# GpSimd's product for the 64-step decay, moved from ahead of the first block's presets to the front of the first half unit

## The chip, the cores and the metric

The kernel runs on one core of one Trainium2 chip. The metric is the device time of one execution in microseconds (us). Three runs of the kernel before gave 900.84 to 903.03 us, with a median of 901.47 us.

## What is computed

A linear attention with decay feeds two feed-forward layers. The inputs have 4 batches, 8 heads, 768 time steps and a head width of 48.

```python
for t in range(S):
    cur = np.einsum('bhd,bhe->bhde', u[None] * kt, vt)
    y[:, :, t] = np.einsum('bhd,bhde->bhe', rt, state + cur)
    state = w[None, :, :, None] * state + np.einsum('bhd,bhe->bhde', kt, vt)
x = y as [3072 tokens, 384]
h = x @ w_in;  g = max(h, 0) + alpha * min(h, 0);  x = g @ w_out      # 384 -> 2048 -> 384
h = x @ w_in2; g = h * tanh(softplus(h));          out = g @ w_out2
```

## The kernel before

**The stages.** Time is cut into six blocks of 128 steps. A block over four batches makes 512 tokens, which is one block of the first feed-forward layer (`mA_h`, `mA_g`, `mA_hi`, `mA_lo`, `mA_out`, 16 slices of the hidden width each). All matrices are split into a high and a low part, and each product is made in three passes. The first block of the attention is worked in four whole units, one per batch (units 0 to 3). From unit 4 on, a unit is a half unit: 64 steps of two batches (`batch`). The second layer follows when all blocks of the first are done.

**A first unit u** goes through these steps. `prep_rk` scales r and k by powers of the decay (DVE). `c_first` makes the diagonal term (DVE, PE, and a copy `cc` on ACT, L385). `scores` makes k times r into two PSUM banks `sc` that all units share (PE, L432). `preset_first` writes the diagonal into a new tile A (POOL, L413). `masked` copies the scores above the diagonal over it (DVE, L436). `attend0` multiplies by v (PE, L447). `x_first` and `x_first_lo` split the result into `x` (ACT L154, DVE L157). `prep_kn` scales k for the state (POOL, L400), and `states_first` sums the states (PE, L509). The A tiles have two homes, so unit 2's waits for unit 0's to be read. The scores of a unit overwrite those that `masked` of the unit before it reads.

**The tables.** `tables` (L291) makes the powers `RK` on DVE. `load_RKs` (L328) copies them by four DMAs into `RKs`, with the heads in other seats. `RKs` is read by `prep_pair` (DVE, L370), which scales r and k of the half units, and by `tables_seat` (POOL, L326): one product of 112x4 elements. Its result `w64` is the decay of 64 steps. Only `t_decay` reads it (DVE, L491), first for unit 4.

```python
    def tables_seat():
        pool.tensor_tensor(out=w64, in0=RKs[:, 1, :, 0], in1=RKs[:, 0, :, HC + 1], op=ALU.mult)
...
        pool.affine_select(out=A_t[u].rearrange("s q p t -> s (q p) t"), in_=c_t[u][1].to_broadcast([128, H, C]),
...
        at(-100.4, tables_seat)
```

**What sets the order.** Each step is entered with `at(place, work)`. `run_plan` (L767) sorts all steps by place and issues them; the table `PLACES` (L59) replaces the place of the steps that it names. Every engine works through its own instructions in that order, so an instruction that waits holds up all behind it on its engine. SP issues the DMAs in the same way, with at most eight unfinished. `tables_seat` has no entry in the table, so its place is -100.4 (L843): behind `scale_Kn` (L336, -100.9) and ahead of `preset_first 1` (-99.35). Also on POOL are `prep_c` (L391, L392: the diagonal term of a half unit, whose sum over elements is `prep_c2` on DVE, L396), `half_tables` (L250, L252: tables for the half units, which overwrite the mask), the casts `w_hi` of every other weight slice (L197), and a memset of a column of the state T in `batch` (L467). `keep_warm` (L563) is filler on PE.

Of the kernel before, what the change touches and what calls it, by code (L numbers as in the profile page):

```python
# [53 lines left out]
def more_state(u):  # L54
# [30 lines left out]
    "load_unit 6": -5.5762, "w_scale (0,3)": -4.4549, "prep_kn 4": -4.4525, "prep_pair 4 1": -3.9618,  # L85
    "mA_h 1": -2.7838, "w_join (0,3)": -2.4808, "w_hi (0,2) False": -2.3395, "scores 4": -1.6028,
# [8 lines left out]
    "prep_c 6": 3.5188, "w_hi (0,5) True": 3.5446, "more_raw 9": 3.6703, "mA_h 4": 3.6974, "mA_out 2": 3.943,  # L95
    "w_lo (0,5)": 3.9878, "w_join (0,6)": 4.1777, "mA_hi 3": 4.1987, "prep_pair 6 1": 4.2457, "mA_lo 3": 4.2643,
    "mA_g 4": 4.3425, "more_raw 10": 4.4486, "w_scale (0,7)": 4.4891, "mA_hi 4": 4.6577, "w_join (0,7)": 4.7254,
    "w_hi (0,6) False": 4.845, "mA_lo 4": 4.9016, "masked 5 1": 5.0498, "w_hi (0,7) True": 5.081, "mA_h 5": 5.1059,
# [12 lines left out]
    "more_raw 14": 9.6065, "w_join (0,11)": 9.6182, "mA_g 9": 9.6854, "w_hi (0,11) True": 9.6935,  # L111
# [7 lines left out]
    "mA_h 12": 12.3428, "mA_g 12": 12.3703, "batch 7": 12.4094, "more_raw 16": 12.4248, "w_hi (0,13) True": 12.4403,  # L119
    "w_lo (0,13)": 12.6061, "w_hi (0,14) False": 12.7117, "mA_hi 12": 12.8951, "x_parts 7": 12.9656,  # L120
    "w_scale (0,15)": 13.0176, "mA_out 11": 13.1742, "mA_h 13": 13.2486, "w_lo (0,14)": 13.4007, "mA_h 14": 13.4763,
    "w_join (0,15)": 13.506, "w_hi (0,15) True": 13.7554, "mA_lo 12": 13.8955, "mA_g 13": 13.8982,
# [865 lines left out]
```

## Time and profile before

| what | value |
|---|---|
| median of three runs | 901.47 us (900.84 to 903.03) |
| the profiled execution's own time | 903.24 us |
| its span, first to last instruction | 901.5 us |
| TensorE busy | 877.4 us (97%) |
| VectorE, ScalarE, GpSimd busy | 632.3, 612.6, 97.0 us |
| mean granted clock of TensorE | 0.989 of full |

An engine's busy time is the time in which it has an instruction at work; for TensorE (PE) the ends of matmuls are modelled. "Granted clock" is the share of the full TensorE clock that the chip allowed. In the timeline, a row is one instruction or a merged run of them: start, length, engine, line, operation, output from input, and in brackets how long the engine was idle before it and what ended that.

### The profile page before, as it was taken

Reading aid. Unit: us, or ns where it says so; the run is one execution under the profiler, and the core shown is the slowest. Engines: PE = TensorE matmul, PEld = TensorE weight load, DVE = VectorE, ACT = ScalarE, POOL = GpSimd, SP = SyncE. Lnnn points to the kernel's source line nnn. Section 1 sums busy time; section 2 is a strip of 40 time slices with the busy share of each in tenths; the row PEclk is TensorE's granted clock in tenths of the full one; section 3 lists DMA queues with packets and bytes.
Section 4 is the critical chain, followed back from the end, with each engine's and each line's share of the span. In section 5 each row is a group of like instructions: output and inputs, shape, how many; then the busy total and the mean of one; then the engine's idle time right before and its main releaser. Section 6 shows DMA issues by size and latency. Waiting matters only on the chain.

```text
span 901.5 us, 17129 instructions
## 1 busy us (share of the span) xinstructions
PE 877.4 (97%) x6700; PEld 758.2 (84%) x6700; DVE 632.3 (70%) x1024; ACT 612.6 (68%) x1159; POOL 97.0 (11%) x119
## 2 busy tenths in 40 slices
PE   9389999999999999999999999999999999999998
PEld 8368878888888888888888899999989989998997
DVE  6198867656565665654665787787787787787875
ACT  2177656444554445543555798898898998998985
POOL 2352222111211122100001000000000000000000
PEclk9699999999999999999999999999999999999999
DMA  8933664435525525231431200200100100100100
GB/s 304 275 98 140 209 139 148 140 102 178 146 73 187 166 91 156 97 105 62 159 105 53 105 1 1 71 1 1 71 1 1 71 0 1 36 1 1 36 1 35
DMA packets 34016, 80.41 MB, mean 89 GB/s; under 512 B 5456, under 2 KB 21136, under 8 KB 33936
## 3 DMA queue, kind: packets, MB, share of 16 engines
q1 hardware_dynamic: 33520, 79.33, 27.8%
q8 instruction: 52, 0.85, 0.4%
q14 instruction: 28, 0.23, 0.1%
q10 hardware_dynamic: 416, 0.00, 0.0%
HBM read 61.16 MB, written 15.73 MB: 85 GB/s over the span
## 4 chain that ended last, share of the span: by engine, by line
PE 90%; DMA 3%; DVE 2%; SPq 2%; ACT 1%; issue 1%; POOL 0%; DVEq 0%; POOLq 0%; ACTq 0%
PE h L228 42%; PE acc L611 21%; PE acc L719 10%; PE sc L719 7%; PE yt L719 3%; PE sc L432 1%; DMA ubt<-in_ub 1%; PE sc L477 1%; PE h L463 1%; PE yt L484 1%; DMA RKs<-RK 1%; DMA w13u<-in_nat 1%; PE yt L463 1%; DMA nat<-in_nat 1%; SPq L552 0%
## 5 line engine op out<-in xcount | busy, mean ns | idle before, releaser
L228 PE MATMUL h<-x,w 128*128 128x512 f32 x1728 | 419.1, 392 | 3.0 <-DVE x L157 1.0
L228 PEld LDWEIGHTS h<-x,w 128*128 128x128 f32 x1728 | 323.5, 188 | 72.3 <-DVE w L157 1.6
L611 PE MATMUL acc<-ghi,w 128*128 128x512 f32 x516 | 175.2, 394 | 0.0
L579 ACT ACTIVATE m<-h 128x512 f32<-128x512 f32 x96 | 57.2, 595 | 91.3 <-PE h L228 91.2
L611 PEld LDWEIGHTS acc<-ghi,w 128*128 128x128 f32 x516 | 96.9, 188 | 21.5
L581 DVE SCALAR_TENSOR_TENSOR g<-m,oma,h 128x512 f32<-128x512 f32 x96 | 71.6, 746 | 58.7 <-ACT m L579 57.8
L154 ACT ACTIVATE ghi<-g 128x512 fp32r<-128x512 f32 x86 | 54.2, 630 | 80.3 <-PE acc L611 43.3
L611 PE MATMUL acc<-glo,w 128*128 128x512 f32 x258 | 101.0, 391 | 0.0
L157 DVE TENSOR_TENSOR glo<-g,ghi 128x512 fp32r<-128x512 f32 x86 | 60.2, 699 | 54.3 <-ACT ghi L154 54.2
L719 PE MATMUL acc<-w,ghiB 128*128 128x384 f32 x384 | 98.0, 337 | 0.0
L667 DVE SCALAR_TENSOR_TENSOR a<-ghi,h 128x512 f32<-128x512 f32 x96 | 66.1, 688 | 36.0 <-ACT ghi L664 28.9
L667 DVE SCALAR_TENSOR_TENSOR g<-s,c 128x512 f32<-128x512 f32 x96 | 66.3, 691 | 22.2 <-ACT s L664 19.0
L154 ACT ACTIVATE ghiB<-g 128x512 fp32r<-128x512 f32 x106 | 65.8, 621 | 18.6 <-DVE g L667 8.1
L157 DVE TENSOR_TENSOR gloB<-g,ghiB 128x512 fp32r<-128x512 f32 x106 | 72.7, 686 | 8.1 <-ACT ghiB L154 8.1
L675 ACT ACTIVATE m<-h 128x512 f32<-128x512 f32 x96 | 56.0, 583 | 28.1 <-PE h L228 28.1
L664 ACT ACTIVATE ghi<-m,half 128x512 f32<-128x512 f32 x96 | 69.6, 725 | 3.2
L719 PEld LDWEIGHTS acc<-w,ghiB 128*128 128x128 f32 x384 | 69.8, 188 | 1.3
L664 ACT ACTIVATE glo<-ghi,m 128x512 f32<-128x512 f32 x96 | 68.0, 709 | 0.1
L664 ACT ACTIVATE s<-glo,m 128x512 f32<-128x512 f32 x96 | 68.0, 709 | 0.0
L664 ACT ACTIVATE s<-s,m 128x512 f32<-128x512 f32 x96 | 68.0, 709 | 0.0
L667 DVE SCALAR_TENSOR_TENSOR b<-ghi,a 128x512 f32<-128x512 f32 x96 | 67.4, 702 | 0.1
L667 DVE SCALAR_TENSOR_TENSOR c<-glo,b 128x512 f32<-128x512 f32 x96 | 65.8, 685 | 0.0
(179 smaller groups left out, 1183.5 us busy)
## 6 DMA issues: line engine op xcount, KB each, us to landing
wrawr<-in_w SPq DMA_DIRECT2D x24, 768.0 KB, 6.0
nat<-in_nat SPq DMA_DIRECT2D x40, 288.0 KB, 4.4
w2d<-wj SPq DMA_DIRECT2D x16, 384.0 KB, 2.6
wraw<-w2d SPq DMA_DIRECT2D x16, 384.0 KB, 3.1
rk<-in_rkT SPq DMA_DIRECT2D x40, 128.0 KB, 2.9
x2d<-xo SPq DMA_DIRECT2D x6, 768.0 KB, 3.2
x<-x2d SPq DMA_DIRECT2D x6, 768.0 KB, 4.5
out<-oo SPq DMA_DIRECT2D x24, 192.0 KB, 1.9
```

The source lines that it names most:

```text
L154: act.activation(out=hi, in_=src, func=AF.Copy)
L157: eng.tensor_tensor(out=lo, in0=src, in1=hi.bitcast(F32), op=ALU.subtract)
L228: pe.matmul(h, w_in(layer, f, a, c), x[:, b, c, :], start=(k == 0), stop=(k == 3 * KC - 1))
L432: pe.matmul(sc_t[u][h][HALF[i], o], rk[ROWS[h], 1, j, s], rk[ROWS[h], 0, j, t], start=True, stop=True)
L463: pe.matmul(y[i][64 * q:64 * q + 64, p * HC:(p + 1) * HC], T[ROWS[h], 2 * bp + i, k, :], pair[i][ROWS[h], 0, k, t], start=(r == 0 and not ...
L579: act.activation(out=m, in_=hA[s], func=AF.Relu, scale=-1.0)
L581: dve.scalar_tensor_tensor(out=g, in0=m, scalar=oma[:, f:f + 1], in1=hA.pop(s), op0=ALU.mult, op1=ALU.add)
L611: pe.matmul(acc[0][c], w_out(0, f, a)[:, c * 128:(c + 1) * 128], g[b], start=(f == 0 and k == 0), stop=(f == NF - 1 and k == 2))
L664: act.activation(out=out, in_=in_, func=AF.Square, scale=scale, bias=fin[bias])
L667: dve.scalar_tensor_tensor(out=out, in0=in0, scalar=scalar, in1=in1, op0=op0, op1=ALU.mult)
L675: act.activation(out=bnew("t", n), in_=v["h", n], func=AF.Tanh, scale=0.5)
L719: pe.matmul(acc[1][t][:, :DM], g[a][:, t * C:(t + 1) * C], w_out(1, f, b), start=(f == 0 and k == 0), stop=(f == NF - 1 and k == 2))
```

## The change

`tables_seat` gets an entry in the table of places. The other rows of the table are only wrapped anew.

```diff
-    "w_scale (0,5)": 0.6537, "prep_c2 5": 0.6799, "masked 4 1": 0.6955, "mA_hi 0": 0.8517, "w_lo (0,2)": 1.0042,
-    "mA_lo 0": 1.3093, "mA_g 1": 1.3135, "batch 4": 1.5628, "t_decay 4": 1.7454, "w_scale (0,4)": 1.7967,
+    "tables_seat": 0.3, "w_scale (0,5)": 0.6537, "prep_c2 5": 0.6799, "masked 4 1": 0.6955, "mA_hi 0": 0.8517,
+    "w_lo (0,2)": 1.0042, "mA_lo 0": 1.3093, "mA_g 1": 1.3135, "batch 4": 1.5628, "t_decay 4": 1.7454,
...
```

GpSimd's (POOL's) instructions from the first preset on, before. L413 are the presets (each writes an A tile from its `cc`), L336 is `scale_Kn`, L326 the product, L400 `prep_kn`; the brackets hold the semaphores that an instruction waits for, DMAHW those of DMAs:

```order
L413 AFFINE_SELECT A<-cc 128x1024 [waits Activation_49]
L336 TENSOR_TENSOR m<-RK,w_98 112x512 [waits DVE_49]
L326 TENSOR_TENSOR w_91<-RKs 112x4 [waits DMAHW3_49,DMAHW4_49,DMAHW2_49,DMAHW1_49]
L413 AFFINE_SELECT A<-cc 128x1024 [waits Activation_49]
L400 TENSOR_TENSOR w11u<-w11u,Kn 128x384 [waits DMAHW0_49,Activation_49]
L413 AFFINE_SELECT A<-cc 128x1024 [waits DVE_49,PE_49,Pool_49]
```

The same place after the change:

```order
L413 AFFINE_SELECT A<-cc 128x1024 [waits Activation_49]
L336 TENSOR_TENSOR m<-RK,w_98 112x512 [waits DVE_49]
L413 AFFINE_SELECT A<-cc 128x1024 [waits Activation_49]
L400 TENSOR_TENSOR w11u<-w11u,Kn 128x384 [waits DMAHW0_49,Activation_49]
L413 AFFINE_SELECT A<-cc 128x1024 [waits DVE_49,PE_49,Pool_49]
L400 TENSOR_TENSOR w13u<-w13u,Kn 128x384 [waits DMAHW3_49]
```

The product with its wait for the four DMAs of `RKs` is gone from between the presets of unit 0 and unit 1; nothing else has changed places here.

Where the product stands now on GpSimd, at the first half unit (unit 4), after the change. L391 and L392 are `prep_c 5`, L197 is the cast of the weight slice (0,3), L467 the memset in `batch 4`, the second L400 `prep_kn 5`:

```order
L391 TENSOR_TENSOR nat<-nat,ubt 128x384 [waits DMAHW7_49,DMAHW0_49]
L392 TENSOR_TENSOR nat<-nat 128x384 [waits Pool_49]
L197 CAST w_592<-wj 128x768 [waits DVE_49,PE_49]
L326 TENSOR_TENSOR w_91<-RKs 112x4 [waits DMAHW3_49,DMAHW4_49,DMAHW2_49,DMAHW1_49]
L467 MEMSET T 112x8 [waits PE_49]
L400 TENSOR_TENSOR nat<-nat,Kn 128x384 [waits Pool_49]
```

It has come in between the cast and the memset. The instructions of PE, DVE, ACT and SP keep their order.

## Rows read from the trace of the kernel before

**Rows 1.** The page: the chain that ended last, by line.
```profile
PE h L228 42%; PE acc L611 21%; PE acc L719 10%; PE sc L719 7%; PE yt L719 3%; PE sc L432 1%; DMA ubt<-in_ub 1%; PE sc L477 1%; PE h L463 1%; PE yt L484 1%; DMA RKs<-RK 1%; DMA w13u<-in_nat 1%; PE yt L463 1%; DMA nat<-in_nat 1%; SPq L552 0%
```
**Rows 2.** Waits, 20 to 60 us: total us, times, longest us.
```profile
POOL w L326 <- DMA RKs<-RK: 18.9, 1, 18.9
DVE A L436 <- POOL A L413: 15.3, 1, 15.3
...
PE sc L432 <- DVE A L436: 13.7, 1, 13.7
```
**Rows 3.** Timeline of POOL: start us, us, what, idle before it.
```profile
13.51 2.00 POOL L336 TENSOR_TENSOR m<-RK,w 112x512 f32<-112x512 f32 x1
34.42 0.21 POOL L326 TENSOR_TENSOR w<-RKs 112x4 f32<-112x4 f32 x1 [18.91 <-DMA RKs<-RK]
34.57 1.09 POOL L413 TENSOR_SCALAR_AFFINE_SELECT A<-cc 128x1024 f32<-128x1024 f32 x1
...
37.64 0.99 POOL L400 TENSOR_TENSOR w13u<-w13u,Kn 128x384 f32<-128x384 f32 x1
...
43.99 1.71 POOL L391 TENSOR_TENSOR nat<-nat,ubt 128x384 f32<-128x384 f32 x1
45.78 1.00 POOL L392 TENSOR_TENSOR nat<-nat 128x384 f32<-128x384 f32 x1
...
59.24 0.11 POOL L467 MEMSET T<- 112x8 f32 x1 [0.31 <-PE yt L463]
```
**Rows 4.** Timeline of PE, units 0 to 3.
```profile
18.58 1.10 PE L432 MATMUL sc<-w10u 48*64 48x64 f32 x32
...
20.15 1.53 PE L447 MATMUL yt<-A,w9u 128*64 128x128 f32 x24
...
22.52 0.92 PE L563 MATMUL acc<-ghi 128*128 128x128 f32 x6
37.09 1.99 PE L432 MATMUL sc<-w12u 48*64 48x64 f32 x32 [13.65 <-DVE A L436]
39.01 2.83 PE L447 MATMUL acc<-A,w11u 128*64 128x128 f32 x24
...
44.46 1.10 PE L432 MATMUL sc<-w14u 48*64 48x64 f32 x32
```
**Rows 5.** Stretches on PE: length, busy, granted clock, DMA share, GB/s.
```profile
26.00:27.00 1.00, 0.00 (x0) 0.50 1.11 277
41.00:42.00 1.00, 1.00 (x12) 0.50 1.17 263
59.00:64.00 5.00, 4.55 (x157) 0.66 0.02 5
```
**Rows 6.** Timeline of ACT and DVE, units 0 to 4.
```profile
14.45 0.18 ACT L385 ACTIVATE cc<-acc 128x8 f32<-128x8 f32 x1 [2.38 <-PE acc L383]
...
19.49 0.95 DVE L186 SCALAR_TENSOR_TENSOR wj<-w4r 128x768 uint32<-128x768 uint32 x1
...
20.26 0.55 ACT L349 ACTIVATE Kn<-acc 128x192 f32<-128x192 f32 x2 [0.47 <-PE acc L346]
...
45.67 1.36 DVE L436 COPY_PREDICATED A<-cst,sc 128x512 f32<-128x512 uint32 x2 [0.82 <-PE sc L432]
...
49.71 0.54 DVE L396 TENSOR_REDUCE cc<-nat 128x8 f32<-128x384 f32 x1
...
54.01 0.89 ACT L180 ACTIVATE w7r<-w7r 128x768 f32<-128x768 f32 x1
```
**Rows 7.** The tile RKs, its readers: duration ns min/median/max, first and last start us.
```profile
L370 DVE TENSOR_TENSOR rk<-rk,RKs x20: 1217/1220/1586, 51.1 to 370.3; 112x1024 f32<-112x1024 f32 x20
```
**Rows 8.** DMA issues that began about 24.2 and 29.5 us: KB each, us to landing.
```profile
nat<-in_nat SPq DMA_DIRECT2D x1, 288.0 KB, 4.7
w7r<-in_w SPq DMA_DIRECT2D x1, 768.0 KB, 6.4
```
**Rows 9.** Chain of waits in order of time: start us, us, what.
```profile
66.31 2.04 PE h L228 x9
```

More of the change, by code (lines that the diff above doesn't have):

```diff
@@ L87 @@
     "more_raw 8": -1.1343, "mA_g 0": -0.9587, "masked 4 0": -0.7567, "prep_c 5": 0.0994, "w_hi (0,3) True": 0.1744,
[7 rows of a table removed]
[L95 to L98, printed above, removed]
[12 rows of a table removed]
-    "more_raw 14": 9.6065, "w_join (0,11)": 9.6182, "mA_g 9": 9.6854, "w_hi (0,11) True": 9.6935,
[7 rows of a table removed]
[L119 to L122, printed above, removed]
[7 rows of a table added]
+    "mA_g 3": 3.4249, "prep_c 6": 3.5188, "w_hi (0,5) True": 3.5446, "more_raw 9": 3.6703, "mA_h 4": 3.6974,
[9 rows of a table added]
+    "mA_out 5": 6.8918, "w_scale (0,10)": 7.2771, "w_hi (0,9) True": 7.378, "prep_kn 6": 7.475, "w_lo (0,8)": 7.4937,
+    "prep_c2 7": 7.5216, "mA_h 7": 7.5404, "mA_g 7": 7.6051, "w_lo (0,9)": 7.7949, "mA_hi 7": 7.8303,
+    "mA_out 6": 7.8692, "mA_lo 7": 7.8968, "masked 6 1": 7.9477, "preset 7 0": 7.9953, "mA_h 8": 8.0248,
+    "w_join (0,10)": 8.1006, "mA_g 8": 8.1678, "w_hi (0,10) False": 8.2945, "batch 6": 8.3841, "more_raw 13": 8.5179,
[7 rows of a table added]
+    "w_hi (0,12) False": 11.0336, "prep_kn 7": 11.1836, "mA_out 10": 11.2072, "w_scale (0,13)": 11.3063,
[3 rows of a table added]
+    "w_hi (0,13) True": 12.4403, "w_lo (0,13)": 12.6061, "w_hi (0,14) False": 12.7117, "mA_hi 12": 12.8951,
+    "x_parts 7": 12.9656, "w_scale (0,15)": 13.0176, "mA_out 11": 13.1742, "mA_h 13": 13.2486, "w_lo (0,14)": 13.4007,
+    "mA_h 14": 13.4763, "w_join (0,15)": 13.506, "w_hi (0,15) True": 13.7554, "mA_lo 12": 13.8955, "mA_g 13": 13.8982,
     "load_unit 9": 13.9017, "preset 8 1": 13.9928, "mA_out 12": 14.1785, "mA_hi 13": 14.2658, "masked 8 1": 14.2923,
```

48 rows, old and new, of the table PLACES are left out of this document.

## The prediction

> **What bounds the kernel now.** I read the page first. Its chain by line is nearly all PE, so a change off PE can pay only where PE stands still; but one of its rows is the DMA of RKs, with 1% of the span, about 9 us [rows 1]. Next come the waits of the first 60 us. The longest is POOL's: 18.9 us at L326, the product that the change moves, for that DMA. DVE then waits 15.3 us for a preset of POOL, and PE 13.7 us for DVE [rows 2]. These are not three losses but one, seen on three engines. The timeline of POOL shows how it begins: `scale_Kn` ends at 13.51 + 2.00 = 15.5 us, POOL stands until the product starts at 34.42, and only behind it, at 34.57, comes the preset of unit 1 [rows 3]. PE has finished its filler at 22.52 + 0.92 = 23.4 us and starts unit 2's scores at 37.09 [rows 4]. The product feeds nothing before unit 4. So a small instruction in an in-order queue holds up units 1, 2 and 3. A second loss hangs on it: 26 to 27 us, with PE idle, is granted 0.50 of the clock, and so is 41 to 42 us, when PE is busy again [rows 5]. [...]
>
> **The change, part by part.** No instruction and no DMA is added or taken away, and SP's queue is the same: the four DMAs of RKs are issued when they were. One POOL instruction of 0.21 us [rows 3] goes past three presets, the two `prep_c` and the other work of POOL up to the first half unit.
>
> *The old place.* The preset of unit 1 needs `cc`, ready at 14.45 + 0.18 = 14.6 us [rows 6], so it runs as soon as POOL is free, 15.5 to 16.6. `prep_kn 1` then waits for Kn, at 20.26 + 0.55 = 20.8 [rows 6], and takes 1.0 us as the like product does [rows 3]. On DVE, `masked 1` comes behind a weight step that ends at 19.49 + 0.95 = 20.4; with 1.36 us for the two copies (unit 3's, [rows 6]) it ends at 21.8. PE reaches the scores of unit 2 at 23.4. So the next to be late is nobody's data: **PE's own queue takes over**, with 1.6 us to spare on DVE.
>
> From here I replay PE with lengths at the full clock. Scores of unit 2, 23.4 + 1.1 = 24.5. `attend0 1`, 1.53, to 26.1. `attend0 2`, the same, to 27.6: its tile A became free when unit 0 was read, at 20.15 + 1.53 = 21.7, so its preset runs from about 21.9 to 23.0, and `masked 2` runs beside `attend0 1`, 24.5 to 25.9. Then filler, 0.92, to 28.5. The scores of unit 3 thus start at about 28.4, as merged rows overlap by 0.1, where they started at 44.46 [rows 4]. **That is 16.0 us earlier**: 13.7 us of standing still and 2.3 us from PE's clock (the scores and two `attend0` at half speed). From unit 3 on the order is the old one and most of it hangs on PE or on a full DVE queue, so I move it as a block by 16.0.
>
> *Does the block run into data that can't come earlier?* Four arrivals stay where they are. (1) RKs, seen on POOL at about 34.4 [rows 3]. `prep_pair` of unit 4 started at 51.1 [rows 7] and moves to 35.1: 0.7 us to spare, so this DMA alone caps the gain at 16.7. (2) The inputs of unit 4: the second half lands at 24.2 + 4.7 = 28.9 [rows 8]. `prep_c 4` would start at 43.99 - 16.0 = 28.0 and waits 0.9 us. Its two products last 46.78 - 43.99 = 2.8 us with the gap between [rows 3], so it ends at 31.7, and `prep_c2 4`, which reads it at 49.71 [rows 6], now wants it at 33.7. (3) The raw weights of slice 3 land at 29.5 + 6.4 = 35.9 [rows 8] and are first read at 54.01 - 16.0 = 38.0 [rows 6]. (4) The moved product is done long before `t_decay`.
>
> *The new place.* There the product finds RKs landed and costs 0.21 us. Behind it stands the memset of T, before which POOL was idle for 0.31 us waiting for PE [rows 3]: that idle time covers the product. Without this cover the memset would be 0.2 us later, and behind it PE's products with T.
>
> *What comes back.* POOL's presets and products again run beside a busy DVE. The trace shows a price of such company: `prep_pair` takes 1.22 us as a rule and 1.59 at most, 0.37 more [rows 7]. Most pairs merely move together; up to four new meetings, an estimate, are 1.5 us on DVE, against the 1.6 us of spare time there before unit 2. I take 0 and keep 1.5 for the range. [...]
>
> **Sum.** 0.0 (product) - 13.7 (idle) - 2.3 (clock) = -16.0 us, or -1.8%. Against its own execution: 903.24 - 16.0 = 887.2; that one lies 1.8 us above the median of the runs, so the median goes from 901.47 to **885.5 us**.
>
> The bounds. If PE had its half clock in this stretch all the same, only the idle time would go, 13.7 us: 887.8; with the 1.5 us of contention, 889.3. On the other side, RKs caps the move at 16.7. PE's clock falls once more near 61 us [rows 5], after waits for first weights and scores: 59 to 64 us have a mean clock of 0.66, which is 5 x 0.34 / 0.5 = 3.4 us at half speed [rows 5]; if this dip does not come again, up to half of it, 1.7 us, is won: 901.47 - 16.7 - 1.7 = 883.1. I widen this by 0.5 for the spread of medians: **882.6 to 889.8 us**.
>
> **The rivals.** I count over 0.3% (2.7 us), about what a measurement of this kernel can tell from no change, as a difference.
>
> *The supply takes over.* With everything 16 us earlier, the DMAs become what PE waits for. For it: 26 to 27 us and 41 to 42 us show the DMA engines full, a share above 1 [rows 5], and of the four arrivals one is missed by 0.9 us and one met by 0.7. Against it: the missed one has 2.0 us to spare at its reader. If each arrival came some 5 us later than I read it, the gain would be 11 us: about 890.5. Chance 0.06.
>
> *Slower: the clock stays down.* [...] Chance 0.02. [...]
>
> *Nothing is won.* POOL was not what held unit 1, and another input of the preset or of `masked 1` comes as late as RKs, or the gap opens again before the first slices. Against it: `cc`, the scores and POOL are all there by 20 us [rows 3, 4, 6]. 901.5. Chance 0.02.
>
> **How the numbers follow.** Forecast 0.90, supply 0.06, slower 0.02, nothing 0.02. The first two are faster by over 0.3%, 0.96 together; same 0.02; slower 0.02. The range holds most of the forecast's chance and a part of the supply's.
>
> **What would show it.** In the profile after, the preset of unit 1 starts at about 15.5 us and POOL's long wait for RKs is gone; PE has no gap at 24 to 37 us, and its granted clock stays full there; the scores of unit 3 start near 28.4 and take 1.10 us; `prep_pair` of unit 4 starts near 35, and only there may RKs appear as a releaser, on DVE. The product, at about 43 us, waits for nothing. The replay is wrong if PE waits for `masked 1` after 23.4, and the block's move is wrong if the first slice of the first feed-forward layer or a later landmark has gained other than 16 us. A dip of the clock near 44 to 47 us, in place of that at 61, would say that the dip moved along.

## The result, and the profile after

The median went from 902.19 us (900.84 to 903.03, four runs: the three known before and one more) to **887.77 us** (886.63 to 888.96, four runs). The ratio is 0.9842 with an interval of 0.9822 to 0.9861, so 14.4 us are won where 16.0 were forecast. The median lies inside the forecast range of 882.6 to 889.8 us and 2.3 us above the 885.5 named there; 0.7 us of this is the median of before, which the fourth run moved. Two later measurements of the same kernel gave 888.13 us (0.9840) and 888.35 us (0.9847).

| what | before | after |
|---|---|---|
| the profiled execution's own time | 903.24 us | 888.96 us |
| its span | 901.5 us | 887.2 us |
| TensorE busy | 877.4 us | 875.1 us (99%) |
| span less TensorE busy | 24.1 us | 12.1 us |
| VectorE, ScalarE, GpSimd busy | 632.3, 612.6, 97.0 us | 634.4, 612.7, 95.5 us |
| mean granted clock of TensorE | 0.989 | 0.998 |

The page's chain by line answers to [rows 1]. The DMA of RKs is gone from it; the DMAs that it now shows each carry 1 or 2%.

```profile
PE h L228 41%; PE acc L611 20%; PE acc L719 11%; PE sc L719 8%; PE yt L719 3%; DMA wrawr<-in_w 2%; DMA w6r<-in_w 1%; DMA nat<-in_nat 1%; SPq L552 1%; PE sc L432 1%; SPq L259 1%; PE sc L477 1%; PE h L463 1%; DMA w12u<-in_rkT 1%; PE yt L484 1%
```

POOL's timeline after, to be held against [rows 3]:

```profile
13.21 2.00 POOL L336 TENSOR_TENSOR m<-RK,w 112x512 f32<-112x512 f32 x1
15.17 1.09 POOL L413 TENSOR_SCALAR_AFFINE_SELECT A<-cc 128x1024 f32<-128x1024 f32 x1
20.92 1.00 POOL L400 TENSOR_TENSOR w11u<-w11u,Kn 128x384 f32<-128x384 f32 x1 [4.66 <-ACT Kn L349]
...
29.00 1.00 POOL L391 TENSOR_TENSOR nat<-nat,ubt 128x384 f32<-128x384 f32 x1 [0.84 <-DMA nat<-in_nat]
...
42.82 0.21 POOL L326 TENSOR_TENSOR w<-RKs 112x4 f32<-112x4 f32 x1
43.17 0.11 POOL L467 MEMSET T<- 112x8 f32 x1
```

The preset of unit 1 follows `scale_Kn` at once, at 15.17 us in place of 34.57, and the product waits for nothing at 42.82. PE's timeline, against [rows 4], shows what the early preset does, and then something new:

```profile
23.39 1.10 PE L432 MATMUL sc<-w12u 48*64 48x64 f32 x32
24.43 1.53 PE L447 MATMUL acc<-A,w11u 128*64 128x128 f32 x24
...
28.33 1.10 PE L432 MATMUL sc<-w14u 48*64 48x64 f32 x32
...
45.38 0.22 PE L484 MATMUL yt<-Ah,nat 64*48 64x64 f32 x1
47.52 0.21 PE L484 MATMUL yt<-Ah,nat 64*48 64x64 f32 x1 [1.93 <-issue]
...
48.63 0.52 PE L611 MATMUL acc<-ghi,w 128*128 128x512 f32 x1
48.96 0.61 PE L611 MATMUL acc<-glo,w 128*128 128x512 f32 x1
```

The scores of units 2 and 3 start at 23.39 and 28.33 us, at the full-clock 1.10 us, with no gap ahead of them. But inside `batch 4`, four matmuls before the end of L484, PE stands for 1.93 us. Its waits over the whole run put this at the top, where [rows 2] had the 13.7 us:

```profile
PE yt L484 <- issue: 1.9, 1, 1.9
PE acc L563 <- POOL ghi L822: 1.2, 1, 1.2
```

"Issue" means that the engine waited for nothing that the profile shows: no semaphore, no data. The kernel before has no such row. The clock, against [rows 5], by stretches of PE (length, busy, number, granted clock, DMA share, GB/s after the other engines' columns):

```profile
23.00:33.00 10.00, 10.00 (x199) 9.03 (x199) 5.64 (x8) 4.58 (x9) 6.73 (x10) 1.00 0.94 219
33.00:48.00 15.00, 9.78 (x206) 7.07 (x202) 14.29 (x20) 11.14 (x22) 6.48 (x7) 1.00 1.04 309
49.00:52.00 3.00, 3.00 (x9) 2.32 (x8) 2.44 (x3) 2.96 (x9) 1.54 (x2) 0.50 0.99 279
```

The clock is full up to and through the batch (1.00); then it is at half (0.50), just when the long matmuls of the first slice run (L611: 0.61 us each in place of 0.39). This execution is the slowest of the four: the other three have a mean clock of 0.999 to 1.0 and hold less of such a dip or none, so the median hardly has it. The chain in order of time gives the price of that, after and before; nine matmuls of L611 take 3.84 us where they took 2.28:

```profile
48.70 3.84 PE acc L611 x9
52.54 2.08 PE h L228 x9
```

```profile
64.03 2.28 PE acc L611 x9
```

**Where the time went**, by the start of the same step on PE in the two timelines:

| step | before | after | earlier by |
|---|---|---|---|
| scores of unit 3 (L432) | 44.46 | 28.33 | 16.1 |
| first slice (L228) | 50.00 | 33.86 | 16.1 |
| `batch 4` (L463) | 58.69 | 42.62 | 16.1 |
| first L611 | 63.97 | 48.63 | 15.3 |
| the next L228 | 66.15 | 52.36 | 13.8 |
| last L611 of the first layer | 458.4 | 444.2 | 14.2 |

So the whole difference between forecast and result arises within ten microseconds at unit 4's batch.

### The profile page after: what moved, and what is told of

It reads as the page before. It is cut to its first block, busy times and chain, and to the rows that moved or that the text cites. A ratio compares the mean times of both kernels' runs of the same rounds, so it can differ in the third digit from the quotient of the medians.

```text
span 887.2 us, 17131 instructions
## 1 busy us (share of the span) xinstructions
PE 875.1 (99%) x6700; PEld 755.2 (85%) x6700; DVE 634.4 (72%) x1024; ACT 612.7 (69%) x1159; POOL 95.5 (11%) x119
## 3 DMA queue, kind: packets, MB, share of 16 engines
q1 hardware_dynamic: 33520, 79.33, 28.4%
## 4 chain that ended last, share of the span: by engine, by line
PE 86%; DMA 6%; SPq 3%; DVE 2%; ACT 1%; issue 1%; POOL 0%; DVEq 0%; ACTq 0%; POOLq 0%
PE h L228 41%; PE acc L611 20%; PE acc L719 11%; PE sc L719 8%; PE yt L719 3%; DMA wrawr<-in_w 2%; DMA w6r<-in_w 1%; DMA nat<-in_nat 1%; SPq L552 1%; PE sc L432 1%; SPq L259 1%; PE sc L477 1%; PE h L463 1%; DMA w12u<-in_rkT 1%; PE yt L484 1%
## 5 line engine op out<-in xcount | busy, mean ns | idle before, releaser
L228 PE MATMUL h<-x,w 128*128 128x512 f32 x1728 | 419.0, 391 | 2.8 <-DVE x L157 1.0
L228 PEld LDWEIGHTS h<-x,w 128*128 128x128 f32 x1728 | 323.5, 188 | 72.2 <-ACT w L154 1.2
L611 PE MATMUL acc<-ghi,w 128*128 128x512 f32 x516 | 176.1, 396 | 0.0
L611 PEld LDWEIGHTS acc<-ghi,w 128*128 128x128 f32 x516 | 97.5, 189 | 21.8
L611 PE MATMUL acc<-glo,w 128*128 128x512 f32 x258 | 101.6, 394 | 0.0
```

What stands on the lines that cost most here:

```text
L228: pe.matmul(h, w_in(layer, f, a, c), x[:, b, c, :], start=(k == 0), stop=(k == 3 * KC - 1))
L611: pe.matmul(acc[0][c], w_out(0, f, a)[:, c * 128:(c + 1) * 128], g[b], start=(f == 0 and k == 0), stop=(f == NF - 1 and k == 2))
```

## The experiments

Two things had to be told apart. Is it the arrival of RKs at one waiting instruction that cost the 14 us? And what is the standstill? **My theory for the second: PE runs out of instructions.** The DMA view has a queue named "instruction". Just ahead of the standstill, in 44 to 45 us, the transfers after are these (packets, MB, share of 16 engines' time):

```profile
q1 hardware_dynamic: 212, 0.19, 102.4%
q8 instruction: 1, 0.02, 8.5%
q14 instruction: 1, 0.01, 3.5%
```

The like stretch before, 58.5 to 60 us, has the same instruction packet and no data:

```profile
q8 instruction: 1, 0.02, 3.9%
q14 instruction: 1, 0.01, 2.4%
```

The packet starts at 58.7 us before, together with the batch (58.69), and at 44.6 after, 2 us behind the batch's start (42.62). For the whole run the page has

```profile
q8 instruction: 52, 0.85, 0.4%
```

in both kernels, and PE's 6700 matmuls with 6700 weight loads, divided by 52, are 258 instructions to a packet: 128 matmuls and their loads would be 256. Before, the DMA engines were empty at the batch (a share of 0.01 in 53 to 63 us); moved up by 16 us, it runs beside the loads of unit 6 and of later weights (1.04 in the stretch of 33 to 48 us above). The rivals: PE's sequencer stalls at this place for a reason of its own, or a semaphore that the profile doesn't show.

**1. RKs early, the product in its old place.** On the kernel before, the power tables and the four copies of RKs go to the front of the order.

```diff
-    "tables": -108.7767, "load_k 3": -108.5738, "load_unit 5": -107.0363, "keep_warm 3########": -106.5162,
+    "tables": -113.1, "load_k 3": -108.5738, "load_unit 5": -107.0363, "keep_warm 3########": -106.5162,
...
-    "c_first 0": -103.8641, "load_RKs": -102.7756, "<lambda> 0": -102.6027, "<lambda> 2": -102.1273,
+    "c_first 0": -103.8641, "load_RKs": -113.05, "<lambda> 0": -102.6027, "<lambda> 2": -102.1273,
```

> The kernel before, with the product in its old place, but the tables are entered first and the four DMAs of RKs are issued ahead of unit 4's loads (about 12.6 to 16 us instead of 26.7 to 29.4). Theory: what cost the 14 us was the wait for RKs, not the place as such; RKs land at 20 to 22.5 us, the product runs then, the preset of unit 1 ends by 23.6, masked 1 by 25, and PE stands for at most 1.7 us at 23.4 us. Unit 4's inputs land some 3 us later, about 31.5, which prep_c 4 can just bear. Time 886 to 891. Rival: the place in the queue itself costs; then 899 to 903 as before.

Measured: 891.18 us in one run, just above the 886 to 891 expected, beside 902.09 for the kernel before on that chip. POOL still waits, but only until 23.50:

```profile
23.50 0.20 POOL L326 TENSOR_TENSOR w<-RKs 112x4 f32<-112x4 f32 x1 [7.65 <-DMA RKs<-RK]
```

PE's gap before unit 2's scores shrinks to 2.39 us. The scores take 1.79, between the full-clock 1.10 and the 1.99 of before, so the clock seems to fall in this gap too:

```profile
26.17 1.79 PE L432 MATMUL sc<-w12u 48*64 48x64 f32 x32 [2.39 <-DVE A L436]
```

The product ran 1.0 us later than the latest time that I had put for it (22.5), and the gap, 1.7 us at most by the theory, is longer for that. Most of the gain (10.9 of 14) is had with the product where it was, so it is the wait for the late copies that cost, and not the place as such. The standstill in L484 is here too (1.7 us), with RKs, POOL and the product ordered quite differently.

**2. The product only two presets later**, behind `prep_kn 2` and ahead of the preset of unit 3.

```diff
+    "tables_seat": -96.2,
```

> The product stands between prep_kn 2 and the preset of unit 3. Theory: POOL stands from 24 us until RKs land at 34.4; units 1 and 2 go as after the change, the preset of unit 3 ends at 35.7 instead of 27.2, masked 3 starts at 35.7 instead of 29.5, and the first feed-forward slices come 6 us later than after the change: 892 to 896 us. PE stands still from about 29 to 37 us and its clock falls. Rival: any place behind the preset of unit 1 gives the full gain: 886 to 889.

Measured: 894.28 us in one run, inside the 892 to 896 expected. The wait goes with the product to the next preset, and PE's gap to `attend0 3`:

```profile
37.47 3.22 PE L447 MATMUL h<-A,w15u 128*64 128x128 f32 x23 [6.13 <-DVE A L436]
```

Six microseconds of gap at unit 3 where it was 13.7 at unit 2, and the half clock after it (0.50 in 36 to 42 us). This is in-order waiting: whichever preset stands behind the product is late. The standstill in L484 is not in this run: its loads end at about 52 us, the packet starts at 50.7, just behind the batch's start (50.48), and the matmul that stands still elsewhere comes at 53.65. Yet the clock falls in the batch here (0.50 in 53 to 55 us, 0.86 on the mean of 48 to 60), so such a dip needs no standstill.

**3. Unit 6's loads held back.** On the changed kernel, the ten loads of unit 6 wait on SP behind a small DMA that reads T after `t_decay 4`.

```diff
-    "load_unit 6": -5.5762, "w_scale (0,3)": -4.4549, "prep_kn 4": -4.4525, "prep_pair 4 1": -3.9618,
+    "load_unit 6": 1.76, "hold": 1.75, "w_scale (0,3)": -4.4549, "prep_kn 4": -4.4525, "prep_pair 4 1": -3.9618,
...
+    def hold():
+        dma.dma_start(out=scr, in_=T[0:16, 0, 0, 0:8])
```

> The change, and the ten loads of unit 6 kept back on SP's queue behind t_decay of unit 4 (by a 512-byte DMA that reads T), so that the DMA engines run empty by about 44 us. Theory: PE's standstill of 1.93 us among unit 4's L484 matmuls is a wait for the 16 KB instruction packet, which starts 2 us late at 44.6 us because the engines are full of loads; with empty engines the packet starts within 0.5 us of unit 4's first L463 (about 42.6 us) and the standstill falls under 0.3 us. The clock then has no reason to fall at 49 us. prep_pair of unit 6 waits up to 2 us for the late loads. Rival: the standstill comes from PE, PSUM or a semaphore of the batch itself; then it stays at 1.9 us. Time by the theory 884.5 to 887, by the rival 888 to 890.

Measured: 891.53 us, ratio 0.9874 (0.9856 to 0.9892), above both ranges. The mechanism came as expected: the instruction packet starts at 42.8 us, in 42 to 43 us of this kernel,

```profile
q1 hardware_dynamic: 66, 0.35, 83.9%
q8 instruction: 1, 0.02, 6.2%
```

before the batch (43.08), and the standstill is gone: from the batch's start to the first L611 it is 3.77 us (46.85) in place of 6.01. The time is the worse because I let the loads go too late. The hold is done at 47.5 us, and r and k of unit 6 are then waited for:

```profile
52.67 1.23 DVE L374 TENSOR_TENSOR rk<-rk,RKs 112x1024 f32<-112x1024 f32 x1 [3.50 <-DMA rk<-in_rkT]
```

That comes back on PE as a wait of 3.1 us in the second slice:

```profile
PE acc L615 <- DVE glo L158: 3.1, 1, 3.1
```

**4. Held back for a shorter time**: as 3, but the small DMA reads the product's result w64, which is there earlier.

```diff
+    "load_unit 6": 0.302, "hold": 0.301, "w_scale (0,3)": -4.4549, "prep_kn 4": -4.4525, "prep_pair 4 1": -3.9618,
...
+        dma.dma_start(out=scr, in_=w64)
```

> The change, and unit 6's ten loads kept back on SP's queue by a small DMA that reads the moved product's result (about 43.1 us) instead of T (47.5 us in the run with the hold on T). Theory: the instruction packet of about 42.8 us still finds the DMA engines empty, so PE's standstill in L484 stays under 0.3 us; the first four loads of unit 6 land 4.8 us after the first is issued, as there, so by about 48.4 us, just ahead of prep_pair of unit 6 (48.6 us after the change): DVE waits under 0.5 us, and PE never waits for it. Without standstill and clock dip: 883.5 to 885.5 us, 2 to 4 us under the change alone, which runs beside it. Rival: any hold of these loads costs PE as much as it gives: 887 to 891.

Measured: 887.13 us, ratio 0.9825 (0.9802 to 0.9848), beside 888.13 (0.9817 to 0.9864) for the change on the same chip: a 1 us lead, inside the spread. That is above the 883.5 to 885.5 expected and inside the rival's 887 to 891: the hold costs about what it gives. The standstill is gone here as well, but in this profile the clock falls in the batch without it (0.57 in 45 to 49 us). Slices 3 to 6 start 1.4 us ahead of those in the profile of experiment 5, of which 0.6 are there at the batch already, and the next ones 0.5; `prep_pair` waits 1.36 us for the held loads, and PE loses 1.0 us to DVE later (`g`, L585, at 115 to 130 us).

**5. The change once more**, on that chip.

> The change as it is, once more, for comparison on the same chip: 886.5 to 889 us by both theories. The standstill of PE in L484 of unit 4 is there again, 1.5 to 2.5 us; whether the clock falls behind it varies from run to run.

Measured: 888.13 us (887.82 to 889.97, five runs). The standstill is there in the profile (2.0 us), and the clock does not fall behind it: 1.00 in 49 to 52 us. This profiled execution has a span of 886.1 us, 1.1 less than the first one's 887.2. So the standstill came in each profile of the change, this, the first and that of experiment 8; the dip of the clock after it did not.

**6. A filler of tiny matmuls** moves PE's later instructions within their packets: two groups of 24 matmuls of 32x32, each of them 48 records in the trace, at places -4.0 and 1.5 of the changed kernel.

```diff
+    def tiny(n):
+        t = bank("acc0")
+        for _ in range(n):
+            pe.matmul(t[0:32, 0:32], zz[:, 0:32], zz[:, 0:32], start=True, stop=True)
...
+        at(-4.0, tiny, 24)
+        at(1.5, tiny, 24)
```

> The change, and 2 x 24 tiny filler matmuls (32x32) on PE in two gaps where it waits 0.8 us anyway: ahead of the second feed-forward slice and ahead of unit 4's batch. They write only a bank that is free. Theory: they move PE's instruction stream on by 96 instructions, so the packet that is late is asked for some 1 to 2 us earlier, while PE is still on long matmuls; the standstill of 1.93 us in unit 4's L484 goes, or moves to an earlier instruction and shrinks under 1 us; the clock dip at 49 us goes too. 884.5 to 887 us. Rival: the standstill belongs to L484 itself (a semaphore or a bank); then it stays there with 1.9 us, 888 to 889.

Measured: 892.0 us, ratio 0.9888 (0.9867 to 0.9908), above both ranges and above the change alone. PE's timeline shows more than the time:

```profile
44.37 0.54 PE L432 MATMUL sc<-rk 48*64 48x64 f32 x13
45.72 0.50 PE L432 MATMUL sc<-rk 48*64 48x64 f32 x18 [0.81 <-issue]
...
47.76 0.48 PE L509 MATMUL acc<-w15u 128*48 128x48 f32 x13
51.47 0.40 PE L509 MATMUL acc<-w15u 128*48 128x48 f32 x3 [3.23 <-issue]
```

The standstill has left L484, and there are two of them now. Counted over the trace, what stands between them is 19 of L432, 32 of L477, 16 of L463, 32 of L484, 16 and 13 of L509, together 128 matmuls. The place is set by the count of instructions, not by what the step does: a stall that belongs to a step, or a hidden semaphore, would have stayed with it. Both packets came while loads ran (a share of 0.82 in 50 to 51 us, inside the second standstill); they start at 42.6 and 48.7 us, and PE goes on 3.1 and 2.8 us after; but the second piece is all small matmuls and was used up in 2.3 us, the first in 5.6, so the second standstill is the longer. The fillers themselves took 1.71 us a group, longer than the 0.8 us of idle time that I had meant for them.

**7. The same idea with a better size.** On the changed kernel, the last two groups of `keep_warm` are thirteen 32x32 matmuls (26 records each) instead of three 128x128 (6 records), 40 matmuls more ahead of the batch.

```diff
+    calls = []
     def keep_warm(n):
         t = bank("acc0")
-        for _ in range(n):
-            pe.matmul(t[:, 0:C], zz[:, 0:C], zz[:, 0:C], start=True, stop=True)
+        calls.append(n)
+        small = len(calls) > 9
+        for _ in range(13 if small else n):
+            w = 32 if small else C
+            pe.matmul(t[0:w, 0:w], zz[:, 0:w], zz[:, 0:w], start=True, stop=True)
```

> The change, and the last two groups of PE's filler (at about 29.4 and 33.2 us; 6 matmul records of 0.14 us each) made of 26 records with 32x32 operands instead, which take about as long. No wait, load or other instruction is touched; only PE's instruction stream is 40 matmuls longer ahead of the first feed-forward slice. Theory: PE takes its instructions in pieces of 128 matmuls (256 instructions, 16 KB). After the change a piece ends four matmuls before the end of unit 4's L484; with 40 more it is asked for at the end of the first slice (about 37 us) and ends early in unit 4's batch, when the next has long come, and the one behind it is not needed before the long matmuls. So PE's standstill of 1.9 us goes, without any change to the DMAs, and no other takes its place: first L611 at 46.5 to 47 us instead of 48.6. In time at the end, 0.5 to 2 us under the change, because DVE and ACT take over a part: 885.5 to 887.5. Rival: the pieces have nothing to do with it; standstill and time as after the change.

Measured: **885.72 us** (884.59 to 886.17, five runs), ratio 0.9813 (0.9798 to 0.9828). The instruction packet now comes in 39 to 41 us, beside engines as full as ever,

```profile
q1 hardware_dynamic: 146, 0.80, 99.5%
q8 instruction: 1, 0.02, 3.2%
```

well before the batch, and the batch runs through to the first slice without a stop:

```profile
46.28 0.56 PE L509 MATMUL acc<-w13u 128*48 128x48 f32 x16
47.14 0.50 PE L616 MATMUL acc<-ghi,w 128*128 128x512 f32 x1
```

No wait and no transfer was taken away here: the two groups of filler take 1.01 us each in place of 0.94, and the border of the piece was moved. Its median is the lowest of all; against experiment 4, on another chip, the intervals of the ratios overlap.

**8. The change a third time**, on the chip of experiment 7.

> The change as it is, on the same chip for comparison: 887 to 889 us, standstill of PE in unit 4's L484 of 1.5 to 2.5 us.

Measured: 888.35 us (886.46 to 891.30, four runs), so experiment 7 is 2.6 us faster, and the two sets of runs don't overlap. The standstill of its profile is 2.7 us.

**9. The other way round, with real loads**: can the old order be given a standstill? On the kernel before, unit 6's loads are held until about the time of the batch.

```diff
-    "load_unit 6": -5.5762, "w_scale (0,3)": -4.4549, "prep_kn 4": -4.4525, "prep_pair 4 1": -3.9618,
+    "load_unit 6": -88.9, "hold": -89.0, "w_scale (0,3)": -4.4549, "prep_kn 4": -4.4525, "prep_pair 4 1": -3.9618,
...
+    def hold():
+        dma.dma_start(out=scr, in_=oma)
```

> The kernel before, with unit 6's ten loads kept back by a small DMA that reads oma (written at 52.6 to 53.6 us), so that they run from about 54 to 62 us, when this kernel's DMA engines are otherwise empty. Theory: the instruction packet that came at 58.7 us now starts 1 to 2 us late, and PE stands still in unit 4's L484 for 0.3 to 2 us, as after the change, although the product is in its old place; 902 to 905 us. Rival: the standstill belongs to the change's own order; then none appears here, 901 to 903.

Measured: 900.19 us in one run, below both ranges, beside 904.08 for the kernel before on that chip, and no standstill. But the loads didn't do what they were for: the engines were busy to 0.68 at 56 to 58 us and 0.35 at 58 to 60, and the packet came at 57.5, with the batch's start (57.59), as early as ever. This run decides nothing.

**10. The other way round, with copies nobody reads**: five copies of 768 KB within the chip's memory, behind a small DMA that reads `oma`, start shortly before the batch of the kernel before.

```diff
+    "hold": -1.05, "copies": -1.04, "dma_start##": -113.2767, "dma_start#": -113.115, "load_unit 4": -112.2722,
...
+    def copies():
+        for i in range(5):
+            dma.dma_start(out=junk[i], in_=w2[i].rearrange("p a n -> p (a n)").bitcast(U32))
```

> The kernel before, with five copies of 768 KB each between DRAM tensors, which nobody reads, issued at about 53.5 us on SP (behind a small DMA that reads oma), so that the DMA engines are full while PE works on unit 4's batch. Theory: the instruction packet that came at 58.7 us comes 1 to 3 us late, and PE stands still for 0.5 to 2.5 us in unit 4's L484, in the old order too. Rival: no standstill; it belongs to the change. Time 902 to 906 us by the theory, 901 to 904 by the rival (later loads may be late as well), so the standstill decides, not the time.

Measured: 905.97 us in one run, beside 902.51 for the kernel before. The packet comes in 62 to 63 us, behind the copies, and not at 58.7:

```profile
q1 hardware_dynamic: 23, 0.59, 172.2%
q8 instruction: 1, 0.02, 7.0%
```

And the standstill is there, in the old order, at the same matmul (L493 is L484 here), fourth before the end, somewhat longer than expected:

```profile
64.70 0.21 PE L493 MATMUL yt<-Ah,nat 64*48 64x64 f32 x1 [2.86 <-issue]
```

Full DMA engines at the batch (a share of 1.72 in 62 to 63 us) were enough to make it here. With experiments 3, 6 and 7 the theory stands: the four show that the standstill goes with the late packet and with the count of instructions.

The traces of all runs agree with it, if a piece, the 128 matmuls that one packet would bring, is taken to begin 128 matmuls ahead of the place of the standstill. In the five runs without a standstill whose loads were absent, thin or about to end (before, experiments 2, 3, 4 and 9; a share of 0.01 in 53 to 63 us before, 0.84 in 42 to 43 and 0.12 in 43 to 44 in experiment 3, 0.68 in 56 to 58 in 9), the packet starts 0.8 to 1.8 us after PE enters the piece; where the engines were full or nearly so (the change, 1, 5, 6, 7, 8 and 10; 1.02 in 44 to 45 us in the change, 1.08 in 40 to 44 in 5, 1.00 in 39 to 41 in 7, 1.72 in 62 to 63 in 10), 2.7 to 4.4 us after. In all seven standstills PE goes on 2.6 to 3.2 us after the packet's start. Experiment 7 alone has a late packet (2.7 us) and no standstill: its piece lasts 8.3 us, those that ran out 2.3 to 5.6.

## Why the prediction was right, and where it was off

**The old place: right.** The forecast put unit 1's preset at about 15.5 us, PE at unit 2's scores at 23.4 and unit 3's at 28.4; the rows have 15.17, 23.39 and 28.33. Both terms came: the idle time of 13.7 us, which shrinks with the wait for RKs in experiment 1 and moves with the product in experiment 2, and the 2.3 us of clock (2.4 by the rows: 16.13 between the two starts of unit 3's scores, less 13.70), since the granted clock is 1.00 in 23 to 33 us: unit 2's scores take 1.10 us in place of 1.99, and `attend0 1` takes 1.53 in place of 2.83 [rows 4]. Up to the batch the block has moved by 16.1.

**The four arrivals: right.** `prep_c 4` waits 0.84 us for its input (0.9 was said) and the sum behind it is not late. RKs is not named as a releaser of `prep_pair`, but there was luck in it: its last copy, issued at about 28.9 us, landed at 34.9, 0.6 us later than in the kernel before, and DVE came at 35.18, so 0.3 us were left of the 0.7 forecast. The tile view and DVE's timeline, to be held against [rows 7]:

```profile
L259 SPq DMA_DIRECT2D RKs<-RK x4: 599/645/682, 26.8 to 28.9; - x4
```

```profile
14.41 2.38 DVE L379 TENSOR_TENSOR g<-w12u 112x512 f32<-112x512 f32 x1
...
20.73 1.34 DVE L436 COPY_PREDICATED A<-cst,sc 128x512 f32<-128x512 uint32 x2
...
35.18 1.45 DVE L370 TENSOR_TENSOR rk<-rk,RKs 112x1024 f32<-112x1024 f32 x1
```

**What comes back from POOL beside DVE: right to take 0.** The new meeting is real (L379, below), but `masked 1` ends at 20.73 + 1.34 = 22.1 us and PE asks for it at 23.39.

**The new place: right.** The product runs at 42.82 us. PE waits 0.3 us for the memset behind it, but it did so before as well, and the memset stands 0.55 us behind the batch's start in both.

**The block's move by 16.0: mis-sized.** The step that failed is that from unit 3 on all moves as one. It holds to the batch; from there 14.2 remain. In numbers of the traces: the standstill is 1.93 us of idle time, a term that the prediction's sum does not have; from start to start it costs 2.2 (6.01 us from the batch to the first L611, where experiment 3 needs 3.77). Against it, before's dip of the clock lay on the batch's small matmuls, which now run at full clock (5.28 us before, so 1.5 won); so the first L611 is only 16.1 - 15.3 = 0.8 us late by this measure. Then the dip lies on the first nine L611, 3.84 - 2.28 = 1.6 us. Some 0.4 us comes back in the next slices. The prediction had foreseen a dip that moves along, near 44 to 47; it came at 49 to 52, behind the standstill, on the long matmuls. The balance of the span agrees: TensorE's busy time fell by 2.3 us, as forecast for the clock, and its idle time by 12.0, which is the 13.7 less the 1.9 of the standstill, to 0.2. The 2.3 is in part luck: it holds two dips that about cancel, the old one gone (1.5) and the new one come (1.6). In experiment 5, without the new one, busy time fell by 3.4 us (877.4 to 874.0), and the last L611 stands at 443.0 us, 15.4 earlier than before.

I had listed four arrivals of data and had the full DMA engines in front of me as a reason for the rival of the supply. What I left out is that instructions come over the same engines (queue q8: 52 packets with 0.85 MB, 8.5% of the engines' time in 44 to 45 us), PE's among them as far as the experiments show. The 258 instructions to a packet worked out above agree with the 128 matmuls of experiment 6. In the runs whose DMA engines have room at that point, and in experiment 7, no standstill is seen; where the engines are full and the piece is small matmuls for the most part, PE stands for 0.8 to 3.2 us.

**What stays open.** No row names the reader of queue q8; that it feeds PE is inferred from the sizes, from experiments 3, 6, 7 and 10, and from two counts. With 96 and 40 more matmuls and no other instruction, experiments 6 and 7 have 53 of its packets in place of 52; and in the second half of every run 127 to 128 matmuls of PE lie between two of them on average (111 to 143). When the packet is asked for is not seen either. It would fit, by an estimate of mine from these counts, if PE asked as it enters the piece ahead: 128 matmuls before the standstill is near the end of the scores ahead of the batch, about 41.7 us, and the piece is all small matmuls, gone in some 4 us; in experiment 7 that piece also has long matmuls in it. The 0.8 to 1.8 us of the runs with room fit this too. Why the clock falls after the standstill in some executions and not in others was not tried; experiments 2 and 4 have a dip at the batch without one.

## What to carry to other kernels

A small instruction that waits for a DMA can cost its whole queue (here 0.21 us of work waited 18.9 us on POOL, and PE stood for 13.7): place it behind what doesn't need its result, as far as its own reader allows, and look for the releaser in the chain of waits rather than at busy shares. When work is moved to an earlier time, ask not only which data it now meets but what else uses the DMA engines there: here a piece of small matmuls was used up fastest (2.3 us in experiment 6, where the mixed one of experiment 7 lasts 8.3) and PE stood when the packet came late, and an "issue" wait with an instruction packet behind a full stretch was the sign. Where that happens, moving the border of the piece by a few instructions (40 filler matmuls here, 2.6 us) can do more than moving loads (experiment 3 lost time by it, and the 1 us of experiment 4 is inside the spread).

## What the runs showed of the hardware

**PE's instructions came late, as far as the runs show.** One standstill at a fixed count of instructions cost 1.7 to 2.0 us in experiments 1 and 5 and the first profile, 2.7 in experiment 8, 2.9 in 10, and two of 0.8 and 3.2 in 6, with the DMA engines at a share of 1.02 in the first profile (44 to 45 us) and 1.72 in experiment 10 (62 to 63). Experiment 7 has 1.00 (39 to 41 us) and none.

**GpSimd and VectorE, as if by turns.** The product L379 (two inputs) takes 0.69 us for unit 3, away from POOL's work, and longer for unit 2. The timeline of DVE before:

```profile
14.71 1.34 DVE L379 TENSOR_TENSOR g<-w12u 112x512 f32<-112x512 f32 x1
...
18.88 0.69 DVE L379 TENSOR_TENSOR g<-w14u 112x512 f32<-112x512 f32 x1
```

Unit 2's runs beside `scale_Kn`, which ends at 15.51 [rows 3]; after, it takes 2.38 us beside `scale_Kn` and the preset, which ends at 15.17 + 1.09 = 16.26. It ends 0.54 us after POOL's work in the one (14.71 + 1.34 - 15.51) and 0.53 in the other (14.41 + 2.38 - 16.26): as if it had run only once POOL was done. The forecast's price of 0.37 us for such a meeting was too low; here one cost 1.0 us more, which the spare time on DVE took in.
